# Late attention scores of two head pairs in one visit to the matrix engine's small tiles, and a second buffer for the gate's value

## The chip, the cores and the metric

The kernel runs on one core of one Trainium2 chip. A core has TensorE (PE in the profile: matmuls; PEld is its loading of weights), VectorE (DVE), ScalarE (ACT), GpSimd (POOL) and SyncE (SP), which here only issues transfers. Matmul results land in PSUM, which has eight banks; everything else lives in SBUF. The metric is the device time of one execution in microseconds.

## The reference

Attention over a sliding window of 96 keys plus 8 global ones, with a linear distance bias per head, followed by a two-layer network whose gate is a hard swish:

```python
batch, n_heads, seq, head_dim = (4, 8, 768, 64)
n_global, n_local = (8, 96)
scores = np.matmul(q, k.transpose(0, 1, 3, 2)) / np.sqrt(D)
scores = scores - slopes * dist            # masked unless global or local
a = np.exp(scores - max); a = a / (sum(a) + 1e-09)
x = (a @ v).transpose(0, 2, 1, 3).reshape(3072, 512)
h = x @ w_in                               # 512 x 2048
g = h * np.clip(h + 3.0, 0.0, 6.0) / 6.0
return g @ w_out                           # 2048 x 512
```

Everything is float32. The network's matmuls are made of three products each, of a high and a low part of both sides (names ending in h and l).

## The kernel before

The 3072 rows are eight blocks of 384 rows. A block has four head pairs (two heads side by side), so there are 32 pairs, n = 0 to 31. Attention of a block fills its x (xh, xl: four tiles, one for each pair), and the network then runs over 16 slices f of the hidden dimension: `first` (L172, 12 matmuls into a PSUM bank hp), `gate` (ACT makes g from hp, L183; DVE multiplies with hp, L184), `high` (POOL, or ACT in an early stage, rounds g to gh, L190 and L192), `rest` (DVE, gl = g - gh, L197), and `second` (L204, 9 matmuls, adding into three acc banks).

Up to some 150 us attention of blocks 0 to 2 and the network of blocks 0 and 1 go on while the network's weights are decoded: in steps on DVE (L433, L434, L442, L446, and L439, which writes the low parts w1l and w2l) and ACT (L399, L411, and L450, which writes w1h and w2h). Then comes a stage named "one", in which the third block's last three pairs are done ("late" pairs from here on, n = 9 and up), and the stage "layers": blocks 2 to 7 go through the network, each while attention for the next block is woven in.

The weave: `twos` takes two slices at a time: both `first` with their gates, two yields, both `second` of the slices before, two more yields. So a block has 32 yields, two for each half slice pair, and `attention` hangs work on their numbers ("units"). Unit k with k mod 4 of 0 or 1 stands after two `first`, with 2 or 3 after two `second`. `TURNS = (0, 5, 10, 16)` gives the unit at which each pair's scores are taken. At that unit `packed` runs: 24 matmuls (L877) in tiles of 64 x 32 of the array, into banks s and t (tiles sp, tp; one bank for each head), then for each of three row tiles and both heads `weigh`: DVE adds the bias and finds the least (L906), ACT takes the exponential with its sum (L910). At the same unit the next pair's queries are scaled (POOL, L863) and the load of the pair three further on is issued. Three units later come the sums' reciprocals (L920, L921) and `normalize` (POOL, L930), four and five later `spread` (DVE transposes into the one tile blocks, L952) and `send` (four transfers from blocks to weights, L958). Units 25 and 26 hold the two halves of `weighted`: attention times values (L704) for all four pairs of the block, into hp, xp, tp and sp, then x.

PSUM: three acc banks, two hp banks used in turn, one each of s, t and x. PE, SP and POOL run in the order in which the code is written; DVE's and ACT's order is set by a scheduler, from the dependencies. A buffer pool with one tile makes the next writer wait until the last reader is done; g has such a pool (`gp1`, one tile), and the scored rows n and their sums have one with three (`up`).

Of the kernel before, what the change touches and what calls it, by code (L numbers as in the profile page):

```python
# [9 lines left out]
F32 = mybir.dt.float32  # L10
# [9 lines left out]
P = 128  # L20
NT = 3
TB = NT * P
NTB = S // TB
NPAIR = H // 2
NKT = DM // P
NF = DF // P
BANK = 512
# [14 lines left out]
PW = PREV + NG + GQ  # L42
# [5 lines left out]
EARLY = 9  # L48
ROOMS = 3
TURNS = (0, 5, 10, 16)  # L50
LEAD = 6
# [12 lines left out]
class Kernel:  # L64
# [45 lines left out]
    def common(self, xs, banks):  # L110
        self.xp = self.pool("xp", xs)
        self.w1h, self.w1l, self.w2h, self.w2l = [], [], [], []
        self.gp = self.pool("gp", 4)
        self.lp = self.pool("lp", 3)
        self.gp1 = self.pool("gp1", 1)
        self.ps_h = self.pool("ps_h", banks, PSUM)
# [418 lines left out]
    def banded(self, flag):  # L535
# [12 lines left out]
        with ExitStack() as early, ExitStack() as words:  # L548
# [82 lines left out]
            self.decoded_to(2 * NF - 1)  # L631
        self.up = self.pool("up", 3, side="right")
        self.bp = self.pool("bp", 1, side="right")
# [9 lines left out]
        self.stage = "layers"  # L643
        x, ahead = xs[2], pairs[-1]
        for i in range(2, len(self.blocks)):
# [27 lines left out]
    def rest_of_third(self, x, slices):  # L673

        units = [[] for _ in range(2 * NF)]
        pairs = [Pair(self, n, x, False) for n in range(EARLY, 3 * NPAIR + 1)]
        pairs[0].scale()
        for p, (me, after) in enumerate(zip(pairs, pairs[1:])):
            at = units[3 * p + 1:]
            at[0] += [me.packed, after.scale, lambda me=me: self.load_next(me.n, False)]  # L680
            at[1] += [me.sum_up] + [lambda t=t, me=me: me.normalize(t) for t in range(NT)]
            at[2] += [lambda t=t, me=me: me.spread(t) for t in range(NT)] + [me.send]
        units[2 * slices - 1].append(lambda: list(self.weighted(pairs[:-1])))
        return units, pairs
# [25 lines left out]

    def attention(self, i, x, first):

        units = [[] for _ in range(2 * NF - 2)]
        pairs = [first]
        first.x = x
        for p in range(NPAIR):
            n = i * NPAIR + p
            me, after = pairs[p], Pair(self, n + 1, x, False) if n + 1 < len(self.blocks) * NPAIR else None
            pairs.append(after)
            at = units[TURNS[p]:]  # L720
            at[0] += [me.packed] + [a.scale for a in (after,) if a] + [lambda me=me: self.load_next(me.n, False)]
            at[3] += [me.sum_up, lambda me=me: me.normalize(0), lambda me=me: me.normalize(1)]
            at[4] += [lambda me=me: me.normalize(2), lambda me=me: me.spread(0)]
            at[5] += [lambda me=me: me.spread(1), lambda me=me: me.spread(2), me.send]
        values = self.weighted(pairs[:NPAIR])
        for k in (25, 26):
            units[k].append(lambda: next(values, None))
        return units, pairs[NPAIR]

# [111 lines left out]
class Pair:  # L841
# [22 lines left out]

    def packed(self):


        nc, kk = self.nc, self.k
        self.sums = kk.up.tile([P, 2, 2 * NT], F32, name="sums")
        banks = [kk.bank(b)[:, 0:NT * PW].rearrange("p (t c) -> p t c", t=NT) for b in "st"]  # L870
        keys, queries = kk.loaded(self.n)
        for t in range(NT):
            for g in range(GROUPS):
                own, c = slice(g * GQ, (g + 1) * GQ), t * TG + g * GQ
                for j in range(2):
                    rows = slice(j * D, (j + 1) * D)
                    nc.tensor.matmul(banks[j][own, t], lhsT=queries[rows, t, own], rhs=keys[rows, c:c + PW], start=True, stop=True,  # L877
                                     tile_position=(j * D, g * GQ))
        for t in range(NT):
            self.weigh(t, [bank[:, t] for bank in banks], kk.up.tile([P, 2, PW], F32, name="n"), 0)  # L880

    def scores(self, t):
# [10 lines left out]
        for j in range(2):  # L893
            rows = slice(j * D, (j + 1) * D)
            nc.tensor.matmul(sp[j][:, lo:W], lhsT=queries[rows, t], rhs=keys[rows, c], start=True, stop=True)  # L895
        return lambda: self.weigh(t, sp, e, lo)

    def weigh(self, t, sp, e, lo):
        nc, kk, end = self.nc, self.k, self.end
        for j in range(2):  # L900
            h, i = 2 * self.pr + j, 2 * t + j
            if self.plain:
                d, scale = (kk.p0 if lo else kk.p1)[:, h], PLAIN
            else:
                d, scale = kk.dl[:, 0 if self.first(t) else 1], SLOPES[h]
            nc.vector.tensor_tensor_reduce(out=e[:, j, lo:end], in0=sp[j][:, lo:end], in1=d, op0=ALU.add, op1=ALU.min, scale=scale,  # L906
                                           scalar=3.0e38, accum_out=self.least[:, i:i + 1])
        for j in range(2):
            i = 2 * t + j
            nc.scalar.activation(out=e[:, j, lo:end], in_=e[:, j, lo:end], func=AF.Exp, bias=self.least[:, i:i + 1], scale=-1.0,  # L910
                                 accum_out=self.sums[:, 0, i:i + 1])
        if self.n <= 2:
            kk.held = nc.cur_bb.bb.instructions[-1].name
        self.rows.append(e)

# [147 lines left out]
```

## Time and profile before

| | us |
|---|---|
| median of 3 runs (lowest, highest) | 646.46 (645.92, 646.66) |
| the profiled execution | 646.94 |
| its span, first to last instruction | 645.1 |
| PE busy | 634.7 |
| DVE busy | 355.0 |
| ACT busy | 255.2 |
| POOL busy | 167.4 |
| mean granted clock | 0.999 |

All times of rows are microseconds from the span's start. In a row of the timeline the start comes first, then the duration, the engine, the line, the operation, and what it writes and reads; in brackets stands how long its engine was idle before it and what ended that. In the table by stage, each engine's busy time stands for a stretch, with the number of instructions. Matmuls overlap, so a row's duration is longer than its step to the next row, and the start of one against the start of the next tells what it costs.

### The profile page before, as it was taken

The numbers are of one execution on the slowest core, as the hardware profiler recorded it, in microseconds if no ns is written. First come the engines' busy times: TensorE is split into PE (matmuls) and PEld (weight loads), VectorE is DVE, ScalarE is ACT, GpSimd is POOL, SyncE is SP. The second block draws the span as 40 slices with busy tenths as digits, with TensorE's granted clock in tenths as the row PEclk, the third lists the DMA queues.
The fourth block names the chain that finished last, engine by engine and source line by source line (L and its number), as shares of the span: only waits on it lengthen the run. The fifth ranks groups of instructions, "written<-read, shape, count | busy, mean of one in ns | idle before, by whom it ended". The sixth has DMA issues, their size and how long they took to land.

```text
span 645.1 us, 14438 instructions
## 1 busy us (share of the span) xinstructions
PE 634.7 (98%) x5593; PEld 559.6 (87%) x5593; DVE 355.0 (55%) x1066; ACT 255.2 (40%) x706; POOL 167.4 (26%) x371
## 2 busy tenths in 40 slices
PE   9989999999999999999999999999999999999997
PEld 7768999888888888988888889888889888899985
DVE  5889999996645552355524464245623555223222
ACT  5897877775415321242223232143212522221111
POOL 4668000000422441124302332033311242012100
PEclk9999999999999999999999999999999999999999
DMA  7675454543334421242232242123312311110001
GB/s 281 176 229 175 160 161 134 161 134 129 92 73 145 100 79 32 70 123 71 60 96 75 66 99 51 68 80 86 92 32 68 109 32 32 33 50 1 1 1 54
DMA packets 34334, 59.78 MB, mean 93 GB/s; under 512 B 3280, under 2 KB 21200, under 8 KB 33488
## 3 DMA queue, kind: packets, MB, share of 16 engines
q1 hardware_dynamic: 33968, 58.50, 30.8%
q8 instruction: 46, 0.75, 0.5%
q14 instruction: 32, 0.26, 0.1%
q10 hardware_dynamic: 288, 0.26, 0.1%
HBM read 41.16 MB, written 6.29 MB: 74 GB/s over the span
## 4 chain that ended last, share of the span: by engine, by line
PE 91%; DVE 2%; ACT 2%; DMA 1%; POOL 1%; issue 1%; SPq 0%; POOLq 0%; ACTq 0%; DVEq 0%
PE hp L172 41%; PE acc L204 36%; PE sp L877 2%; PE sp L204 2%; PE tp L204 1%; PE xp L204 1%; PE hp L704 1%; ACT n L910 1%; PE sp L704 1%; DMA wst<-w 1%; POOL n L930 1%; DMA load<-pairs 1%; PE xp L970 1%; PE sp L895 1%; PE tp L704 1%
## 5 line engine op out<-in xcount | busy, mean ns | idle before, releaser
L183 ACT ACTIVATE g<-hp,small 128x384 f32<-128x384 f32 x127 | 73.7, 580 | 259.6 <-PE hp L172 163.9
L172 PE MATMUL hp<-xh,w1h 128*128 128x384 f32 x512 | 173.7, 339 | 0.0
L172 PE MATMUL hp<-xh,w1l 128*128 128x384 f32 x512 | 172.4, 337 | 0.1
L172 PE MATMUL hp<-xl,w1h 128*128 128x384 f32 x512 | 171.7, 335 | 0.0
L190 POOL TENSOR_SCALAR gh<-g 128x384 fp32r<-128x384 f32 x104 | 53.6, 515 | 424.2 <-DVE g L184 397.3
L184 DVE SCALAR_TENSOR_TENSOR g<-g,hp 128x384 f32<-128x384 f32 x128 | 70.7, 552 | 121.0 <-ACT g L183 119.8
L204 PE MATMUL acc<-w2h,gh 128*128 128x512 f32 x336 | 133.2, 397 | 0.0
L204 PE MATMUL acc<-w2l,gh 128*128 128x512 f32 x336 | 131.7, 392 | 0.0
L204 PE MATMUL acc<-w2h,gl 128*128 128x512 f32 x336 | 131.7, 392 | 0.0
L197 DVE TENSOR_TENSOR gl<-g,gh 128x384 fp32r<-128x384 f32 x128 | 71.4, 558 | 78.5 <-POOL gh L190 58.8
L910 ACT ACTIVATE n<-n,least 128x136 f32<-128x136 f32 (+2 forms) x192 | 79.6, 417 | 54.1 <-DVE least L906 53.4
L172 PEld LDWEIGHTS hp<-xh,w1h 128*128 128x128 f32 x512 | 96.1, 188 | 4.7 <-issue 1.9
L172 PEld LDWEIGHTS hp<-xl,w1h 128*128 128x128 f32 x512 | 96.1, 188 | 2.6
L172 PEld LDWEIGHTS hp<-xh,w1l 128*128 128x128 f32 x512 | 96.1, 188 | 0.9 <-DVE w1l L439 0.8
L930 POOL TENSOR_SCALAR n<-n,sums 128x136 f32<-128x136 f32 (+2 forms) x186 | 82.4, 460 | 39.4 <-DVE sums L921 23.6
L204 PEld LDWEIGHTS acc<-w2h,gh 128*128 128x128 f32 x336 | 63.1, 188 | 15.6 <-issue 3.8
L204 PEld LDWEIGHTS acc<-w2h,gl 128*128 128x128 f32 x336 | 63.1, 188 | 13.8 <-DVE gl L197 0.3
L204 PEld LDWEIGHTS acc<-w2l,gh 128*128 128x128 f32 x336 | 63.1, 188 | 11.4
L952 DVE STREAM_TRANSPOSE blocks<-n 128x256 f32<-128x256 f32 x138 | 51.2, 424 | 22.9 <-POOL n L930 21.4
L910 ACT ACTIVATION_READ_ACCUMULATOR n<-n,least 128x1 f32 x192 | 36.2, 188 | 0.0
L399 ACT ACTIVATE wz<-wst 128x512 f32<-128x512 f32 x32 | 21.6, 677 | 6.1 <-DVE w2l L439 3.9
L446 DVE CUSTOM_DVE_ANT_0 wz<-wz,we 128x1024 uint16<-128x1024 uint16 x32 | 22.3, 696 | 1.3 <-POOL we L404 0.9
(126 smaller groups left out, 731.1 us busy)
## 6 DMA issues: line engine op xcount, KB each, us to landing
wst<-w SPq DMA_DIRECT2D x32, 512.0 KB, 3.6
load<-pairs SPq DMA_DIRECT2D x31, 444.0 KB, 3.5
weights<-blocks SPq DMA_DIRECT2D x92, 120.0 KB, 2.4
values<-values SPq DMA_DIRECT2D x6, 1024.0 KB, 4.9
out<-o SPq DMA_DIRECT2D x23, 256.0 KB, 2.4
values<-pairs SPq DMA_DIRECT2D x9, 384.0 KB, 3.9
out<-o ACTq DMA_DIRECT2D x1, 256.0 KB, 2.8
load<-pairs SPq DMA_DIRECT2D x1, 252.0 KB
```

Of the source, the lines that this page charges most:

```text
L172: self.nc.tensor.matmul(hp, lhsT=self.w1(w, f)[:, kt, :], rhs=a[:, kt, :], start=(n == 0), stop=(n == 3 * NKT - 1))
L183: nc.scalar.activation(out=g, in_=hp, func=AF.Relu, bias=self.three, scale=1.0)
L184: nc.vector.scalar_tensor_tensor(out=g, in0=g, scalar=6.0, in1=hp, op0=ALU.min, op1=ALU.mult)
L190: self.nc.gpsimd.tensor_scalar(out=gh, in0=g, scalar1=1.0, scalar2=0.0, op0=ALU.mult, op1=ALU.add)
L197: self.nc.vector.tensor_tensor(out=gl, in0=g, in1=gh.bitcast(F32), op=ALU.subtract)
L204: self.nc.tensor.matmul(acc[tt], lhsT=a[:, tk], rhs=self.w2(w, f), start=(f == 0 and j == 0), stop=(f == NF - 1 and j == 2))
L399: self.nc.scalar.activation(out=self.z[i].bitcast(F32), in_=words[:, :, 1].bitcast(F32), func=AF.Abs)
L446: tt(out=z, in0=z, in1=self.e.pop(i), op=ALU.add)
L704: nc.tensor.matmul(out[pr][j * D:(j + 1) * D, g0 * GQ:g1 * GQ], lhsT=self.values_of[own, c, j * D:(j + 1) * D], rhs=groups[own, j, g0:g1, ...
L910: nc.scalar.activation(out=e[:, j, lo:end], in_=e[:, j, lo:end], func=AF.Exp, bias=self.least[:, i:i + 1], scale=-1.0, accum_out=self.sums ...
L930: nc.gpsimd.tensor_scalar(out=e[:, j, lo:end], in0=e[:, j, lo:end], scalar1=over, scalar2=0.0, op0=ALU.mult, op1=ALU.add)
L952: nc.vector.transpose(out=self.blocks[:, :, t, 4 * s:4 * s + 4], in_=e[:, :, c:c + P].rearrange("p j (b q) -> p j b q", b=4))
```

## The change

`packed` is now called for two pairs in a row. `TURNS` is (2, 10): a block's pairs 0 and 1 at unit 2, pairs 2 and 3 at unit 10. The first of a couple writes an hp bank and the x bank, the second s and t; the first reads its hp bank for all three row tiles before its x bank (`heads`), in reductions and in exponentials. The first pair's normalize, spread and send keep their distance from the unit (3 to 5 later), the second's come two units after that. The queries of both pairs of a couple are scaled beforehand: the next couple's first at the unit of the scores, its second five units later. For that the third block's stage makes one more pair object and scales it. `up` has six tiles instead of three, and `gp1`, the gate's value, two instead of one.

```diff
@@ -47,7 +47,7 @@
 PLAIN = -1 / np.sqrt(D)
 EARLY = 9
 ROOMS = 3
-TURNS = (0, 5, 10, 16)
+TURNS = (2, 10)
 LEAD = 6
 WAKE = 9
 FIRST = 3
@@ -112,7 +112,7 @@
         self.w1h, self.w1l, self.w2h, self.w2l = [], [], [], []
         self.gp = self.pool("gp", 4)
         self.lp = self.pool("lp", 3)
-        self.gp1 = self.pool("gp1", 1)
+        self.gp1 = self.pool("gp1", 2)
         self.ps_h = self.pool("ps_h", banks, PSUM)
 
     def weight_chunk(self, i):
@@ -629,7 +629,7 @@
             for _ in self.halves(todo):
                 pass
             self.decoded_to(2 * NF - 1)
-        self.up = self.pool("up", 3, side="right")
+        self.up = self.pool("up", 6, side="right")
         self.bp = self.pool("bp", 1, side="right")
         self.late_tiles()
         self.op = self.pool("op", 3, side="right")
@@ -641,7 +641,7 @@
         self.finish()
         self.pending = []
         self.stage = "layers"
-        x, ahead = xs[2], pairs[-1]
+        x, ahead = xs[2], pairs[-2:]
         for i in range(2, len(self.blocks)):
             units, x_next = [], None
             if i + 1 < len(self.blocks):
@@ -673,14 +673,15 @@
     def rest_of_third(self, x, slices):
 
         units = [[] for _ in range(2 * NF)]
-        pairs = [Pair(self, n, x, False) for n in range(EARLY, 3 * NPAIR + 1)]
+        pairs = [Pair(self, n, x, False) for n in range(EARLY, 3 * NPAIR + 2)]
         pairs[0].scale()
-        for p, (me, after) in enumerate(zip(pairs, pairs[1:])):
+        for p, (me, after) in enumerate(zip(pairs[:-2], pairs[1:])):
             at = units[3 * p + 1:]
             at[0] += [me.packed, after.scale, lambda me=me: self.load_next(me.n, False)]
             at[1] += [me.sum_up] + [lambda t=t, me=me: me.normalize(t) for t in range(NT)]
             at[2] += [lambda t=t, me=me: me.spread(t) for t in range(NT)] + [me.send]
-        units[2 * slices - 1].append(lambda: list(self.weighted(pairs[:-1])))
+        at[4].append(pairs[-1].scale)
+        units[2 * slices - 1].append(lambda: list(self.weighted(pairs[:-2])))
         return units, pairs
 
     def weighted(self, pairs):
@@ -708,24 +709,26 @@
             self.put_x(pairs[0].x, pr, out[pr])
         self.load_values(block + 1)
 
-    def attention(self, i, x, first):
+    def attention(self, i, x, pairs):
 
         units = [[] for _ in range(2 * NF - 2)]
-        pairs = [first]
-        first.x = x
-        for p in range(NPAIR):
-            n = i * NPAIR + p
-            me, after = pairs[p], Pair(self, n + 1, x, False) if n + 1 < len(self.blocks) * NPAIR else None
-            pairs.append(after)
-            at = units[TURNS[p]:]
-            at[0] += [me.packed] + [a.scale for a in (after,) if a] + [lambda me=me: self.load_next(me.n, False)]
-            at[3] += [me.sum_up, lambda me=me: me.normalize(0), lambda me=me: me.normalize(1)]
-            at[4] += [lambda me=me: me.normalize(2), lambda me=me: me.spread(0)]
-            at[5] += [lambda me=me: me.spread(1), lambda me=me: me.spread(2), me.send]
+        for pair in pairs:
+            pair.x = x
+        pairs = pairs + [Pair(self, n, x, False) for n in range(i * NPAIR + 2, min(i * NPAIR + 6, len(self.blocks) * NPAIR))]
+        for p in range(0, NPAIR, 2):
+            couple, after = pairs[p:p + 2], pairs[p + 2:p + 4]
+            at = units[TURNS[p // 2]:]
+            at[0] += [lambda me=me, first=first: me.packed(first) for me, first in zip(couple, (True, False))]
+            at[0] += [a.scale for a in after[:1]] + [lambda me=me: self.load_next(me.n, False) for me in couple]
+            at[5] += [a.scale for a in after[1:]]
+            for k, me in enumerate(couple):
+                at[2 * k + 3] += [me.sum_up, lambda me=me: me.normalize(0), lambda me=me: me.normalize(1)]
+                at[2 * k + 4] += [lambda me=me: me.normalize(2), lambda me=me: me.spread(0)]
+                at[2 * k + 5] += [lambda me=me: me.spread(1), lambda me=me: me.spread(2), me.send]
         values = self.weighted(pairs[:NPAIR])
         for k in (25, 26):
             units[k].append(lambda: next(values, None))
-        return units, pairs[NPAIR]
+        return units, pairs[NPAIR:]
 
 
     def general_setup(self):
@@ -862,12 +865,13 @@
         _, q = kk.loaded(self.n)
         nc.gpsimd.tensor_scalar(out=q, in0=q, scalar1=kk.over[:, self.pr:self.pr + 1], scalar2=0.0, op0=ALU.mult, op1=ALU.add)
 
-    def packed(self):
+    def packed(self, first=False):
 
 
         nc, kk = self.nc, self.k
         self.sums = kk.up.tile([P, 2, 2 * NT], F32, name="sums")
-        banks = [kk.bank(b)[:, 0:NT * PW].rearrange("p (t c) -> p t c", t=NT) for b in "st"]
+        banks = [kk.ps_h.tile([P, BANK], F32, name="hp"), kk.bank("x")] if first else [kk.bank("s"), kk.bank("t")]
+        banks = [bank[:, 0:NT * PW].rearrange("p (t c) -> p t c", t=NT) for bank in banks]
         keys, queries = kk.loaded(self.n)
         for t in range(NT):
             for g in range(GROUPS):
@@ -876,8 +880,10 @@
                     rows = slice(j * D, (j + 1) * D)
                     nc.tensor.matmul(banks[j][own, t], lhsT=queries[rows, t, own], rhs=keys[rows, c:c + PW], start=True, stop=True,
                                      tile_position=(j * D, g * GQ))
-        for t in range(NT):
-            self.weigh(t, [bank[:, t] for bank in banks], kk.up.tile([P, 2, PW], F32, name="n"), 0)
+        self.rows = [kk.up.tile([P, 2, PW], F32, name="n") for _ in range(NT)]
+        for heads in ((0,), (1,)) if first else ((0, 1),):
+            for t in range(NT):
+                self.weigh(t, [bank[:, t] for bank in banks], self.rows[t], 0, heads)
 
     def scores(self, t):
         nc, kk = self.nc, self.k
@@ -893,11 +899,12 @@
         for j in range(2):
             rows = slice(j * D, (j + 1) * D)
             nc.tensor.matmul(sp[j][:, lo:W], lhsT=queries[rows, t], rhs=keys[rows, c], start=True, stop=True)
+        self.rows.append(e)
         return lambda: self.weigh(t, sp, e, lo)
 
-    def weigh(self, t, sp, e, lo):
+    def weigh(self, t, sp, e, lo, heads=(0, 1)):
         nc, kk, end = self.nc, self.k, self.end
-        for j in range(2):
+        for j in heads:
             h, i = 2 * self.pr + j, 2 * t + j
             if self.plain:
                 d, scale = (kk.p0 if lo else kk.p1)[:, h], PLAIN
@@ -905,13 +912,12 @@
                 d, scale = kk.dl[:, 0 if self.first(t) else 1], SLOPES[h]
             nc.vector.tensor_tensor_reduce(out=e[:, j, lo:end], in0=sp[j][:, lo:end], in1=d, op0=ALU.add, op1=ALU.min, scale=scale,
                                            scalar=3.0e38, accum_out=self.least[:, i:i + 1])
-        for j in range(2):
+        for j in heads:
             i = 2 * t + j
             nc.scalar.activation(out=e[:, j, lo:end], in_=e[:, j, lo:end], func=AF.Exp, bias=self.least[:, i:i + 1], scale=-1.0,
                                  accum_out=self.sums[:, 0, i:i + 1])
         if self.n <= 2:
             kk.held = nc.cur_bb.bb.instructions[-1].name
-        self.rows.append(e)
 
     def sum_up(self, t=None):
```

PE, at the first excursion of the stage "layers" (sp, tp, hp and xp are banks, load_72 and load_73 two pairs' keys and queries). Before:

```order
L172 MATMUL hp<-xh,w1l_145 128x384
L877 MATMUL sp<-load_72 32x136
L877 MATMUL tp<-load_72 32x136
...
L172 MATMUL hp<-xh,w1h_144 128x384
...
L877 MATMUL sp<-load_73 32x136
L877 MATMUL tp<-load_73 32x136
```

And now:

```order
L172 MATMUL hp<-xh,w1l_145 128x384
L881 MATMUL hp<-load_72 32x136
L881 MATMUL xp<-load_72 32x136
...
L881 MATMUL sp<-load_73 32x136
L881 MATMUL tp<-load_73 32x136
L172 MATMUL hp<-xh,w1h_144 128x384
```

The second pair's 24 matmuls follow the first's with no large matmul between.

DVE, at the end of the decoding, from the gate of slice 14 on (wz and we are the decoded chunk's tiles, w1l_1029 the low part of the first layer's weights for slice 15). Before:

```order
L433 TENSOR_SCALAR wz<-wz 128x512
L446 ISA wz<-wz,we 128x1024
L184 SCALAR_TENSOR_TENSOR g<-g,hp 128x384
L434 TENSOR_SCALAR wz<-wz 128x512
L439 TENSOR_TENSOR w1l_1029<-wz,w1h_1028 128x4x128
L442 SCALAR_TENSOR_TENSOR wz<-wst,wz 128x512
L197 TENSOR_TENSOR gl<-g,gh 128x384
```

And now:

```order
L184 SCALAR_TENSOR_TENSOR g<-g,hp 128x384
L446 ISA wz<-wz,we 128x1024
L433 TENSOR_SCALAR wz<-wz 128x512
L197 TENSOR_TENSOR gl<-g,gh 128x384
L434 TENSOR_SCALAR wz<-wz 128x512
L439 TENSOR_TENSOR w1l_1029<-wz,w1h_1028 128x4x128
L442 SCALAR_TENSOR_TENSOR wz<-wst,wz 128x512
```

The gate and gl stand ahead of decoding steps that they stood behind.

DVE, at the end of a block's attention (the last pair's transposes into blocks, then the gates of the slices up to the block's x, which `weighted` ends). Before:

```order
L184 SCALAR_TENSOR_TENSOR g<-g,hp 128x384
L197 TENSOR_TENSOR gl<-g,gh 128x384
L952 STREAM_TRANSPOSE blocks<-n 128x2x128 x2
L184 SCALAR_TENSOR_TENSOR g<-g,hp 128x384
L197 TENSOR_TENSOR gl<-g,gh 128x384
L184 SCALAR_TENSOR_TENSOR g<-g,hp 128x384
L197 TENSOR_TENSOR gl<-g,gh 128x384
L159 TENSOR_TENSOR xl<-hp,xh 128x384
```

And now:

```order
L197 TENSOR_TENSOR gl<-g,gh 128x384
L958 STREAM_TRANSPOSE blocks<-n 128x2x128 x2
L184 SCALAR_TENSOR_TENSOR g<-g,hp 128x384
L197 TENSOR_TENSOR gl<-g,gh 128x384
L184 SCALAR_TENSOR_TENSOR g<-g,hp 128x384
L197 TENSOR_TENSOR gl<-g,gh 128x384
L184 SCALAR_TENSOR_TENSOR g<-g,hp 128x384
L197 TENSOR_TENSOR gl<-g,gh 128x384
L184 SCALAR_TENSOR_TENSOR g<-g,hp 128x384
L197 TENSOR_TENSOR gl<-g,gh 128x384
L159 TENSOR_TENSOR xl<-hp,xh 128x384
```

Between the last transposes and x stand four gates instead of two.

## The prediction

> **What bounds the kernel now.** I read the page's busy shares and costliest groups first, then the table by stage, then TensorE's rows one by one, start against start.
>
> ```profile
> span 645.1 us, 14438 instructions
> PE 91%; DVE 2%; ACT 2%; DMA 1%; POOL 1%; issue 1%; SPq 0%; POOLq 0%; ACTq 0%; DVEq 0%
> L172 PE MATMUL hp<-xh,w1h 128*128 128x384 f32 x512 | 173.7, 339 | 0.0
> 198.00:570.00 372.00, 372.00 (x3800) 328.50 (x3799) 176.20 (x581) 109.41 (x352) 101.54 (x219) 1.00 0.27 71
> ACT g L183 <- DVE gl L197: 77.7, 39, 2.9
> ```
>
> From 198 to 570 us, where the change mainly acts, TensorE (PE) is busy for all 372 us at full clock; VectorE (DVE), ScalarE (ACT) and GpSimd (POOL) are at half or less. So only what shortens PE's own sequence counts. The last row is what the second g tile removes: 77.7 us of ACT waiting for gl. It pays nothing by itself, since PE waits for none of it.
>
> A modelled busy row hides short holes, so I compare starts.
>
> **Term 1, the merged excursions.** These are starts of a slice pair (594.44 to 602.75 without scores, 267.66 to 277.05 with one pair's scores), then the first and last score rows and the next large matmul.
>
> ```profile
> 594.44 0.33 PE L172 MATMUL hp<-xh,w1h 128*128 128x384 f32 x1
> 602.75 0.33 PE L172 MATMUL hp<-xh,w1h 128*128 128x384 f32 x1
> 267.66 0.33 PE L172 MATMUL hp<-xh,w1h 128*128 128x384 f32 x1
> 277.05 0.33 PE L172 MATMUL hp<-xh,w1h 128*128 128x384 f32 x1
> 271.94 0.30 PE L877 MATMUL sp<-load 64*32 64x136 f32 x1
> 272.63 0.28 PE L877 MATMUL tp<-load 64*32 64x136 f32 x1
> 272.84 0.50 PE L204 MATMUL acc<-w2h,gh 128*128 128x512 f32 x1
> 257.42:259.26 1.84, 1.84 (x130) 1.80 (x129) 0.00 (x0) 0.00 (x1) 0.00 (x0) 1.00 0.00 0
> ```
>
> A pair of slices takes 8.31 us, with scores 9.39: an excursion costs 1.08. Its 48 records (24 matmuls, two each) begin between 271.94 and 272.63, 0.69 us; the other 0.39 is entry and exit. A second pair that follows at once in free banks needs the 0.69 and no entry or exit. That the pace holds for twice as long I take from the value matmuls: some 128 records in 1.84 us, 14 ns each, as in a score burst (0.69/48). The twenty late pairs become ten excursions: 10 x 0.39 = **-3.9 us**. The other end: the second pair costs the full distance from first score to next large matmul, 0.90; then 1.08 - 0.90 = 0.18 is saved, 1.8 in all. I take 3.9, since nothing stands between the two pairs: no wait on PE, banks hp, xp, sp and tp all free.
>
> A rule speaks against this term. The Trainium skill, page "TensorEngine Tiling (Array Packing)", section Instruction Overhead, gives each matmul some 60 cycles however short it is; at the 2.4 GHz of "Trainium Kernel Development and Optimization", NeuronCore Architecture, that is 25 ns, my estimate for 48 records in a row is 1.2 us, more than an excursion now, and the merge would lose 0.1 each time, 1 us in all. The trace's 14 ns do not agree: the eight array tiles overlap.
>
> **Term 2, the values' wait.** Per block, the values' matmuls come as two bursts, after units 25 and 26. The first:
>
> ```profile
> 232.59 0.30 PE L877 MATMUL sp<-load 64*32 64x136 f32 x1
> 245.53 0.77 DVE L952 STREAM_TRANSPOSE blocks<-n 128x256 f32<-128x256 f32 x2 [0.56 <-POOL n L930]
> 246.33 2.56 SPq L958 DMA_DIRECT2D weights<-blocks  x4
> L704 PEld LDWEIGHTS sp<-weights,values x32: 127/131/133, 250.8 to 252.8; 32*64 32x64 f32 x32
> L704 PEldq EVENT_SEMAPHORE  x1: 706/706/706, 250.1 to 250.1; - x1
> 250.31 0.54 PE L704 MATMUL tp<-weights,values 32*64 32x384 f32 x2
> 250.87 0.54 PE L704 MATMUL sp<-weights,values 32*64 32x384 f32 x2
> 326.10:328.45 2.35, 2.35 (x97) 1.92 (x97) 1.04 (x2) 0.58 (x1) 0.41 (x1) 1.00 0.00 1
> 332.80:334.42 1.62, 1.62 (x114) 1.58 (x113) 0.00 (x0) 0.01 (x1) 0.00 (x0) 1.00 0.00 0
> 190.57:193.82 3.25, 3.25 (x158) 2.89 (x157) 0.48 (x1) 0.00 (x0) 0.00 (x0) 1.00 0.03 5
> ```
>
> The fourth pair's matmuls (tile sp) start 0.56 us after the third's (tp), where 0.02 would do; PE's sequencer sat 0.71 in a wait. What came late is that pair's send: its last transposes end at 246.30, the four DMAs are issued from 246.33 and land some 4.5 us behind the transposes, at 250.8. Second witness: 13 chunks take 3.25 us in the one burst at 190.57 (three pairs, but the tiles of all pairs run side by side, so a chunk takes as long), and 2.35 + 1.62 = 3.97 in the two at 326.10 and 332.80; a second exit is 0.2 (272.63 to 272.84), so 0.5 is the wait. Now the fourth pair's scores stand at unit 10, not 16. From that excursion to the values' first burst lie 1.8 + 3 x 8.31 + 4.2 = 30.9 us instead of 17.7 (232.59 to 250.3); its spread and send come at units 16 and 17, behind only the slices 8 and 9 gates, and by the chain below land near 23 us: 8 to spare. Five blocks x 0.5 = **-2.5 us** (ends 1.5, if the chunks behind the wide one absorb part, and 3.0).
>
> **Term 3, the decode's last slices.** Until 152 us DVE both decodes weights and serves the gates, almost without a gap. The second g tile lets the scheduler set some gates earlier in DVE's order, and decoding steps move with them.
>
> ```profile
> PEld hp L172 <- DVE w1l L439: 0.8, 2, 0.4
> 136.77 0.34 PE L172 MATMUL hp<-xl,w1h 128*128 128x384 f32 x1
> 137.18 0.44 PE L172 MATMUL hp<-xh,w1l 128*128 128x384 f32 x1
> 147.60 0.58 ACT L183 ACTIVATE g<-hp,small 128x384 f32<-128x384 f32 x1 [1.00 <-PE hp L172]
> 148.19 0.62 ACT L450 CAST w1h<-wz 128x512 fp32r<-128x512 f32 x1
> 147.13 0.42 DVE L433 TENSOR_SCALAR wz<-wz 128x512 f32<-128x512 f32 x1
> 147.47 0.68 DVE L446 CUSTOM_DVE_ANT_0 wz<-wz,we 128x1024 uint16<-128x1024 uint16 x1
> 148.21 0.56 DVE L184 SCALAR_TENSOR_TENSOR g<-g,hp 128x384 f32<-128x384 f32 x1
> 148.68 0.42 DVE L434 TENSOR_SCALAR wz<-wz 128x512 int32<-128x512 int32 x1
> 149.02 0.69 DVE L439 TENSOR_TENSOR w1l<-wz,w1h 128x512 fp32r<-128x512 f32 x1
> 149.44 0.34 PE L172 MATMUL hp<-xh,w1h 128*128 128x384 f32 x1
> ```
>
> PE waits twice for w1l today (slices 10 and 13), 0.8 in the row, 0.24 by the matmul starts 136.77 and 137.18 where 0.17 is the step; I take 0.35 each. In the new order both w1l stand ahead of gl or of a decode step (0.5 to 0.6 us): **-0.7**. For slice 15 it turns over. The gate of slice 14 now stands ahead of the decode step L446; it cannot begin before ACT's g ends (148.18), so DVE, whose L446 began at 147.47, now idles till then, runs g to 148.68 (0.47 from start to start) and L446 to 149.37; the cast w1h on ACT (0.62) follows: w1h is there near 150.0 instead of 148.8, while PE wants it at 149.44, 0.6 late. w1l now comes behind L446, L433, gl and L434 (0.6, 0.34, 0.47, 0.34 by starts, gl taken as long as g) and ends near 151.1 against 149.71; PE, already 0.6 behind, wants it two matmuls later, at 150.4: another 0.7. **+1.3** (ends: 0, if DVE's chain starts enough earlier than PE's, and 2).
>
> **Edits costed at nothing.** The same 23 query scalings (POOL), loads, sends and reductions are issued, only elsewhere. On SP two loads go in a row ahead of eight sends; the sends wait for transposes anyway. What is new is a long ACT and DVE job per excursion: twelve reductions and twelve exponentials, behind which both gates stand.
>
> ```profile
> 276.37 1.54 ACT L60 ACTIVATE o<-acc 128x512 f32<-128x512 f32 x3
> L910 ACT ACTIVATE n<-n,least 128x136 f32<-128x136 f32 (+2 forms) x192 | 79.6, 417 | 54.1 <-DVE least L906 53.4
> 303.52 2.57 POOL L930 TENSOR_SCALAR n<-n,sums 128x136 f32<-128x136 f32 x6
> L952 DVE STREAM_TRANSPOSE blocks<-n 128x256 f32<-128x256 f32 x138 | 51.2, 424 | 22.9 <-POOL n L930 21.4
> 273.61 0.29 DVE L906 CUSTOM_DVE_ANT_0 n<-sp,dl 128x136 f32<-128x136 f32 x1
> 273.82 0.29 DVE L906 CUSTOM_DVE_ANT_0 n<-tp,dl 128x136 f32<-128x136 f32 x1
> ```
>
> From the first excursion's start: three o copies on ACT to 1.6, twelve exponentials at 0.4 to 6.4, sums and both gates on DVE to 7.9. The next slice that wants the gate's bank starts at 1.8 + 8.3 = 10.1 us: 2.2 to spare. Then on POOL two gh and six n (2.57) to 11.6, transposes to 12.2; the first pair's send frees the blocks tile 4.5 later, 16.7; the second pair's six transposes (0.37 apart by the rows above) with a gate and a gl between end near 19.9. Only then DVE reads the scores of the second excursion, which began at 18.4. Its hp bank is read first, three reductions of 0.22, done at 20.6; the slice that wants that bank starts at 18.4 + 1.8 + 2.1 = 22.3. Cover 1.7 us, in each block's second excursion; without it, every us beyond costs five.
>
> **Sum.** -3.9 - 2.5 - 0.7 + 1.3 = -5.8 us. The profiled execution took 646.94 us (1.8 of it outside the span), so 641.1; the median of the runs, 646.46, lies 0.48 below it, so I forecast **640.7 us**.
>
> **Rivals.**
> - *The second pair of an excursion does not run at the first one's pace* (0.90 instead of 0.69): 1.8 saved, 642.8 us. For it: nowhere in the trace do 96 such score records follow each other. Against it: the long value bursts keep 14 ns. Chance 0.10. By the rule of the page on tiling, an estimate, the time would end near 645.7; since 14 ns per record is measured, I leave it 0.01 of the 0.10.
> - *The wait ahead of the fourth pair's values stays*, because something other than the send ends it: 640.7 + 2.5 = 643.2. For it: the row names no releaser. Against it: the send's end and the wait's end agree to a tenth. Chance 0.10.
> - *DVE's new order costs more*: two further gates (slices 9 and 12) also moved ahead; if each held decode up as slice 14's does, +2.6, 643.3. Against it: of sixteen w1l the wait row above names two, so the others have slack now. Chance 0.08.
> - *The other side: the second excursion's hp bank comes free late.* DVE is in order: the second pair's first transpose waits for the first pair's send, and gates, reductions and PE stand behind it. It decides from 1.7 us of lateness; from 1.7 + 5.8/5 = 2.9 us it eats the whole gain. Were a send to need 8 us instead of 4.5, it would cost 5 x 1.8 = 9: 649.7. For it: the loads and the next sends share SP's queue. Against it: the four DMAs of a block's pair took the same 4.5 us in the row above. Chance 0.05.
> - *The change moves nothing on PE* (banks or scalings not ready, the couple split again): 646.5. PE's order speaks against it. Chance 0.03.
>
> **How the numbers follow.** My own case has the remaining 0.64, with a range from 639.5 (no new decode wait, value wait 0.6) to 642. The range 639.5 to 643.4 takes in the first three rivals. 0.2% (1.3 us) is about what a measurement of this kernel tells from no change: faster than 645.2 are my case and the first three rivals, 0.92; within it the last, and a milder bank wait, 0.04; slower than 647.7 is the bank rival, 0.04.
>
> **What the profile after would show.** Ten late excursions, their score rows about 1.4 us from first to last; slice-pair starts 8.31 + 1.79 apart around them (a 2.0 means the first rival). The value bursts 2.35 and 2.75 shrink to some 1.85 and 2.25, the sequencer's wait at L704 is gone. No w1l wait near 115 and 136 us, but one near 149, 1.3 together on w1h and w1l. No PE hole two slices after a block's second excursion: such a hole, on DVE's reductions, would make the prediction wrong, and so would sends that land after 30 us.

## Result and the profile after

The changed kernel takes 642.80 us (median of 4 runs, 641.78 to 643.03) against 646.42: a ratio of 0.9937, 95% interval 0.9924 to 0.9949, so 3.6 us less. The forecast was 640.7, from 639.5 to 643.4: right in sign and within the range, 2.1 us too low. The profiled execution took 643.03 with a span of 641.2, 3.9 less than the 645.1 before; the forecast was 5.8 less.

Two rows of the page of the changed kernel, one of its table by stage, and two of its list of waits:

```profile
span 641.2 us, 14374 instructions
L172 PE MATMUL hp<-xh,w1h 128*128 128x384 f32 x512 | 174.2, 340 | 0.5 <-ACT w1h L450 0.5
```

```profile
198.00:570.00 372.00, 372.00 (x3829) 332.91 (x3828) 176.57 (x583) 108.91 (x354) 103.99 (x219) 1.00 0.26 72
```

```profile
ACT g L183 <- PE hp L172: 252.4, 91, 5.7
DVE blocks L958 <- DMA weights<-blocks: 22.4, 11, 2.4
```

PE is still busy throughout the stage; it now starts more matmuls in the same 372 us (3829 against 3800). ACT's gate no longer waits for gl at all (89.5 us in the whole execution before), and but for one wait of 2.0 us for POOL it waits for PE alone. Two things are new: an idle time of PE for w1h, and DVE's transposes waiting 22.4 us for sends (1.5 before).

The merged excursion, from the timeline (first score, first and last of the second pair, next large matmul, and the starts of the slice pairs around two excursions):

```profile
267.66 0.33 PE L172 MATMUL hp<-xh,w1h 128*128 128x384 f32 x1
276.06 0.30 PE L881 MATMUL hp<-load 64*32 64x136 f32 x1
276.78 0.28 PE L881 MATMUL sp<-load 64*32 64x136 f32 x1
277.47 0.28 PE L881 MATMUL tp<-load 64*32 64x136 f32 x1
277.67 0.44 PE L172 MATMUL hp<-xh,w1h 128*128 128x384 f32 x1
286.09 0.33 PE L172 MATMUL hp<-xh,w1h 128*128 128x384 f32 x1
```

The second pair follows without a gap and takes 0.69 us, as the first; first to last score are 1.41 us. From 267.66 to 286.09 are two slice pairs and one excursion: 18.43 = 2 x 8.31 + 1.81. Two single excursions cost 2.16, so one merged saves 0.35, and ten save 3.5.

The values' first bursts, in the table by stage, in the rows of L705 (L704 before) and in PE's timeline:

```profile
250.72:253.07 2.35, 2.35 (x130) 1.89 (x129) 1.03 (x2) 0.58 (x1) 0.51 (x1) 1.00 0.00 0
325.40:327.41 2.01, 2.01 (x97) 1.55 (x96) 1.04 (x2) 0.58 (x1) 0.51 (x1) 1.00 0.00 0
```

```profile
L705 PEld LDWEIGHTS sp<-weights,values x32: 127/131/132, 250.8 to 252.8; 32*64 32x64 f32 x32
L705 PEldq EVENT_SEMAPHORE  x8: 51/51/51, 247.5 to 250.5; - x8
250.76 0.54 PE L705 MATMUL sp<-weights,values 32*64 32x384 f32 x2
```

The sequencer's 706 ns are gone, and sp starts with the other three tiles (hp, the first of them, at 250.72). The first bursts take 2.35, 2.01, 2.35, 2.01 and 2.35 us instead of 2.79, 2.35, 2.73, 2.38 and 2.74: 1.9 in all.

Slice 15 of the decode, in the timelines of DVE, ACT and PE:

```profile
147.94 0.55 DVE L184 SCALAR_TENSOR_TENSOR g<-g,hp 128x384 f32<-128x384 f32 x1 [0.60 <-ACT g L183]
148.41 0.68 DVE L446 CUSTOM_DVE_ANT_0 wz<-wz,we 128x1024 uint16<-128x1024 uint16 x1
149.13 0.62 ACT L450 CAST w1h<-wz 128x512 fp32r<-128x512 f32 x1
149.80 0.45 PE L172 MATMUL hp<-xh,w1h 128*128 128x384 f32 x1 [0.47 <-ACT w1h L450]
150.16 0.68 DVE L439 TENSOR_TENSOR w1l<-wz,w1h 128x512 fp32r<-128x512 f32 x1
150.89 0.44 PE L172 MATMUL hp<-xh,w1l 128*128 128x384 f32 x1 [0.48 <-DVE w1l L439]
```

As forecast, DVE idles for ACT's g, L446 slips behind the gate, w1h and then w1l come late, and PE stands twice.

Since PE runs the network's matmuls in the same order in every kernel here, the start of the same matmul in two traces says where time went. From the slice that starts at 115.37 us before to the one at 198.08 (82.71 us), the changed kernel needs 0.83 more; from there to the last slice's start (198.08 to 633.27, 435.19 us) it needs 429.82, so 5.37 less. The rest, 0.6, is lost ahead of 115 us (0.3) and behind the last slice's start (0.4), which the forecast did not touch. The first of these two is one late transfer, in ACT's timeline:

```profile
52.46 0.66 ACT L399 ACTIVATE wz<-wst 128x512 f32<-128x512 f32 x1 [2.20 <-DMA wst<-w]
```

Here ACT waits 2.20 us for raw weights, and PE falls 0.7 behind (of which it had been 0.4 ahead). The same wait is 2.5 and 2.6 in two of the kernels below, 0.5 to 1.3 in five, and absent in four and before. Up to this row ACT, DVE and POOL have their instructions in the same order in all of these kernels, and two kernels that both have two g tiles from the start have the wait short and long (0.5 in two_g_alone, 2.6 in two_banks), so I take it for a matter of the execution. It was not tried by itself.

### The profile page after: what moved, and what is told of

Its sections match the earlier page's. It is cut to its first block, busy times and chain, and to the rows that moved or that the text cites. A ratio compares the mean times of both kernels' runs of the same rounds, so it can differ in the third digit from the quotient of the medians.

```text
span 641.2 us, 14374 instructions
## 1 busy us (share of the span) xinstructions
PE 628.5 (98%) x5593; PEld 557.5 (87%) x5593; DVE 354.1 (55%) x1066; ACT 253.7 (40%) x706; POOL 169.8 (26%) x371
## 4 chain that ended last, share of the span: by engine, by line
PE 90%; DVE 4%; ACT 2%; DMA 2%; POOL 1%; issue 1%; POOLq 0%; ACTq 0%
PE hp L172 42%; PE acc L204 36%; PE sp L204 2%; PE tp L204 2%; PE xp L204 2%; PE hp L705 1%; ACT n L917 1%; PE hp L881 1%; DVE n L913 1%; DMA wst<-w 1%; PE xp L705 1%; DMA iv<-bounds 1%; POOL n L936 1%; PE tp L705 1%; PE tp L881 1%
## 5 line engine op out<-in xcount | busy, mean ns | idle before, releaser
L204 PE MATMUL acc<-w2h,gh 128*128 128x512 f32 x336 | 131.6, 392 | 0.0
L184 DVE SCALAR_TENSOR_TENSOR g<-g,hp 128x384 f32<-128x384 f32 x128 | 69.4, 548 | 99.4 <-ACT g L183 98.4
L197 DVE TENSOR_TENSOR gl<-g,gh 128x384 fp32r<-128x384 f32 x128 | 73.8, 582 | 76.5 <-POOL gh L190 39.2
L936 POOL TENSOR_SCALAR n<-n,sums 128x136 f32<-128x136 f32 (+2 forms) x186 | 84.3, 473 | 17.2 <-DVE sums L927 12.3
L958 DVE STREAM_TRANSPOSE blocks<-n 128x256 f32<-128x256 f32 x138 | 51.6, 422 | 31.9 <-DMA weights<-blocks 22.4
L446 DVE CUSTOM_DVE_ANT_0 wz<-wz,we 128x1024 uint16<-128x1024 uint16 x32 | 22.1, 692 | 1.4 <-POOL we L404 0.9
```

The source lines that it names most:

```text
L184: nc.vector.scalar_tensor_tensor(out=g, in0=g, scalar=6.0, in1=hp, op0=ALU.min, op1=ALU.mult)
L197: self.nc.vector.tensor_tensor(out=gl, in0=g, in1=gh.bitcast(F32), op=ALU.subtract)
L204: self.nc.tensor.matmul(acc[tt], lhsT=a[:, tk], rhs=self.w2(w, f), start=(f == 0 and j == 0), stop=(f == NF - 1 and j == 2))
L446: tt(out=z, in0=z, in1=self.e.pop(i), op=ALU.add)
L936: nc.gpsimd.tensor_scalar(out=e[:, j, lo:end], in0=e[:, j, lo:end], scalar1=over, scalar2=0.0, op0=ALU.mult, op1=ALU.add)
L958: nc.vector.transpose(out=self.blocks[:, :, t, 4 * s:4 * s + 4], in_=e[:, :, c:c + P].rearrange("p j (b q) -> p j b q", b=4))
```

## Experiments

Each kernel was profiled once and timed. Columns: median; ratio to the kernel before, which was timed anew beside each group (medians 646.64, 647.12 and 646.67), with its 95% interval; then, from starts of the same matmuls in its profile, the length of the end of decoding (115.37 to 198.08 before) and of the stretch with the late excursions (198.08 to 633.27 before).

| kernel | us | ratio | end of decoding | late stretch |
|---|---|---|---|---|
| before | 646.46 | 1 | 82.71 | 435.19 |
| changed | 642.80 | 0.9937 (0.9924 to 0.9949) | 83.54 | 429.82 |
| one_g | 642.61 | 0.9935 (0.9918 to 0.9952) | 82.68 | 430.88 |
| two_g_alone | 646.05 | 0.9991 (0.9979 to 1.0002) | 83.56 | 433.18 |
| turn14 | 645.36 | 0.9976 (0.9966 to 0.9986) | 82.71 | 433.29 |
| split | 646.03 | 0.9990 (0.9981 to 1.0000) | 83.57 | 433.67 |
| g2_late | 641.80 | 0.9922 (0.9909 to 0.9935) | 82.74 | 430.06 |
| one_g_wide | 642.93 | 0.9938 (0.9925 to 0.9951) | 82.69 | 431.39 |
| two_banks | 664.45 | 1.0282 (1.0261 to 1.0303) | 83.58 | 450.66 |
| one_burst | 649.67 | 1.0042 (1.0026 to 1.0057) | 82.73 | 435.96 |
| one_g_212 | 641.64 | 0.9924 (0.9911 to 0.9938) | 82.72 | 429.82 |
| g2_late_212 | 641.50 | 0.9923 (0.9910 to 0.9937) | 82.74 | 429.59 |
| heads_together | 642.47 | 0.9936 (0.9922 to 0.9949) | 83.55 | 430.10 |

The fourth column reads by itself: five of five kernels with two g tiles during decoding lose 0.83 to 0.87 us there, and the seven others lose nothing.

**split: the merging undone.** Changed kernel, with

```
-            at[0] += [lambda me=me, first=first: me.packed(first) for me, first in zip(couple, (True, False))]
+            at[0] += [lambda me=couple[0]: me.packed(True)] + ...
+            at[2] += [lambda me=couple[1]: me.packed(False), ...]
```

> The changed kernel with a couple's second pair scored two units later (after the next two firsts instead of right behind the first pair), its load with it; banks, sums, normalize, spread and send stay where they are. Theory: ten entries and exits of the small tiles come back at 0.35 each: +3.5 against the changed kernel, 646.3; a slice pair with its excursion is again 8.31 + 1.08 long, and the score rows 0.69 from first to last. The value bursts stay as in the changed kernel. Rival: the merging itself saves little (0.1 to 0.18 each, the other end of my term), and the gain comes from earlier sends: 644 to 644.6. If nothing hangs on the merging, 642.8.

```profile
269.12 0.33 PE L172 MATMUL hp<-xh,w1h 128*128 128x384 f32 x1
287.90 0.33 PE L172 MATMUL hp<-xh,w1h 128*128 128x384 f32 x1
```

These are the starts around two slice pairs with two single excursions, in its timeline: 18.78 us against the changed kernel's 18.43. The late stretch is 3.85 longer, of which 0.4 is a wait for a g behind the very first excursion, so 3.4 belongs to the merging: ten times 0.34. By the two ratios to the kernel before it is 0.0053 of that time, 3.4 us. The theory holds; the other end (1.8 in all) does not. The bursts are those of the changed kernel (2.35 and 2.01).

**turn14: the last pair's send earlier, nothing merged.** Kernel before, with

```
-TURNS = (0, 5, 10, 16)
+TURNS = (0, 5, 10, 14)
...
-        self.up = self.pool("up", 3, side="right")
+        self.up = self.pool("up", 6, side="right")
```

> The kernel before with its last pair's scores at unit 14 instead of 16 (and six tiles instead of three for n and sums, which the overlap of two pairs needs), so that its send goes out at unit 19 instead of 21, some 4 us earlier. No pairs are merged. Theory: the values' wait was for that send; PE's sequencer wait at L704 goes and each block's first burst is 0.38 us shorter, 5 x 0.38 = 1.9 us less: 644.5. Rival: the wait is ended by something else (the values' load, the hp bank): the 0.71 stays and the time is 646.4.

The late stretch is 1.90 shorter, the first bursts are 2.35 and 2.01, and all semaphore waits of L704 in the first block's values are 51 ns. By the runs it is 0.9976, 1.6 us less. The values' wait was for that send.

**two_g_alone: the second g tile without the rest.** Kernel before, with

```
-        self.gp1 = self.pool("gp1", 1)
+        self.gp1 = self.pool("gp1", 2)
```

> The kernel before with two tiles for the gate's value, nothing else. Theory: +1.4 at slice 15 and -0.5 at slices 10 and 13, nothing after 198 us: 0.9 us slower than before, 647.3. Rival: two tiles help PE in the stage from 198 to 570 us (ACT waits 77.7 us for gl there): faster than before by over 1 us. Third way: the stall near 51 to 54 us belongs to it: 648.

Both halves of the table were needed to read it. The end of decoding is 0.85 longer, as the theory has it, but the late stretch is 2.01 shorter, which the theory had at zero. The rows of L704, and two of DVE's timeline, say where:

```profile
L704 PEld LDWEIGHTS sp<-weights,values x32: 128/131/132, 251.1 to 253.1; 32*64 32x64 f32 x32
L704 PEldq EVENT_SEMAPHORE  x8: 51/51/184, 247.8 to 250.8; - x8
```

```profile
243.44 0.56 DVE L184 SCALAR_TENSOR_TENSOR g<-g,hp 128x384 f32<-128x384 f32 x1 [0.19 <-ACT g L183]
245.81 0.77 DVE L952 STREAM_TRANSPOSE blocks<-n 128x256 f32<-128x256 f32 x2 [0.28 <-POOL n L930]
```

The wait for the fourth pair's values is 184 ns instead of 706, the burst 2.34 instead of 2.79. PE is 0.75 behind the kernel before at that place, yet the last transposes begin only 0.28 later: the second gate no longer waits for the first gl, POOL gets to gh and n earlier, and the send leaves some half a microsecond earlier against PE. So two parts of the change remove the same wait, and either is enough.

**one_g: the changed kernel with one g tile.**

```
-        self.gp1 = self.pool("gp1", 2)
+        self.gp1 = self.pool("gp1", 1)
```

> The changed kernel with one tile for the gate's value instead of two; the merged excursions and the new turns stay. Theory: the second tile only moves gates in the decode and pays nothing later. Then the wait at slice 15 (1.4 us near 147 to 152 us) goes, the two waits for w1l at 115 and 136 us (0.25 each) come back, and the stage from 198 to 570 us keeps its length: 0.9 us less than the changed kernel, some 641.9. Rival: the second tile is what lets both gates behind twelve exponentials finish in time; with one, the second g waits for the first gl, and PE stalls some 0.5 us two slices after each of ten excursions: +5, some 647, with idle time of PE on DVE g (L184) there. Third way: the stall near 51 to 54 us (0.7 us, ACT waiting for a load of weights) hangs on the second tile too; then 641.2.

The 0.86 of the decode come back, and 1.06 are lost in the late stretch: together nothing. So the theory misses the late stretch, and the rival misses size and place. The loss is in the first two blocks. PE's timeline, DVE's and the waits, at the first block's second excursion (scores from 218.56):

```profile
218.92 0.45 DVE L958 STREAM_TRANSPOSE blocks<-n 128x256 f32<-128x256 f32 x1 [2.25 <-DMA weights<-blocks]
221.55 0.77 DVE L958 STREAM_TRANSPOSE blocks<-n 128x256 f32<-128x256 f32 x2 [0.28 <-POOL n L936]
222.25 0.26 DVE L913 CUSTOM_DVE_ANT_0 n<-hp,dl 128x136 f32<-128x136 f32 x1
222.66 0.29 DVE L913 CUSTOM_DVE_ANT_0 n<-hp,dl 128x136 f32<-128x136 f32 x1
222.20 0.34 PE L172 MATMUL hp<-xh,w1l 128*128 128x384 f32 x1
223.10 0.41 PE L172 MATMUL hp<-xh,w1h 128*128 128x384 f32 x1 [0.57 <-DVE least L913]
```

This is the chain of the prediction's rival of the other side: the second pair's transposes wait for the first pair's send, DVE reads the excursion's hp bank only behind them (the last of three reductions ends at 222.95), and PE, which would want the bank at 222.4, goes on at 223.10. It costs 0.7 and 0.3 in two blocks. The changed kernel has no such hole, but two g tiles alone don't rule it out: g2_late and heads_together below have one each. What the changed kernel has to spare there, from the last reduction's end to the slice that takes the bank, is 0.57 and 0.71 in these two blocks and 1.7, 1.7 and 1.6 in the other three; the prediction had 1.7 in each.

**one_g_wide and one_g_212: is it the distance of the excursions?** one_g with

```
-TURNS = (2, 10)
+TURNS = (0, 10)        # one_g_wide
+TURNS = (2, 12)        # one_g_212
```

> The changed kernel with one g tile throughout and TURNS (0, 10) instead of (2, 10): the two excursions of a block stand ten units apart instead of eight, 4.2 us more. Theory: the holes of one_g come from the first couple's first send (DVE's transposes of the second pair wait 2.2 us for it, and the reductions that free the excursion's hp bank stand behind them); with 4.2 us more the send has landed, both holes (1.2 in sum) go, and PE's starts gain that against one_g: some 641.4. Rival: the holes come from the gates behind twelve exponentials with one g tile, which the distance does not touch: 642.6 as one_g.

That missed. The second block's hole is gone, but the first block's grew. At the first block no `second` is pending, so units 0 and 2 are the same place of PE's order and its two excursions stand no further apart (199.89 and 218.50). And there DVE's timeline shows another chain:

```profile
217.73 2.08 DVE L958 STREAM_TRANSPOSE blocks<-n 128x256 f32<-128x256 f32 x6 [4.02 <-DMA weights<-blocks]
219.73 0.51 DVE L197 TENSOR_TENSOR gl<-g,gh 128x384 fp32r<-128x384 f32 x1
220.95 0.56 DVE L184 SCALAR_TENSOR_TENSOR g<-g,hp 128x384 f32<-128x384 f32 x1 [0.71 <-ACT g L183]
```

All six transposes wait 4.02 us for the send, gl stands behind them, ACT's g waits for gl (one tile), and PE waits 1.4 us for g. Hence the second try, which leaves the first excursion where it was:

> The changed kernel with one g tile throughout and TURNS (2, 12): the first excursion stays where it is, the second comes after the next two firsts, so that the slice which wants its hp bank is some 4 us further off (5.5 us of cover by one_g_wide's excursions at such a place, against 0.15 in one_g's first two blocks). Theory: one_g's holes are the hp bank of the second excursion, freed late because DVE's reductions stand behind transposes that wait for a send; they go in both blocks, 1.2 in sum: PE's starts at 631 us some 1.2 earlier than in one_g, the time some 641.4, and a second g tile is worth nothing any more. Rival, from one_g_wide, whose first block lost 1.4 us to a gl that stood behind those transposes: with one g tile the gate chain itself waits for the send, wherever the excursion is; then a hole near 220 us stays, on g or gl, and the time is 642.6.

Both holes are gone: the late stretch is 1.06 shorter than one_g's, 429.82, as long as the changed kernel's, and the time 641.64. The holes were a matter of distance; with it, the second g tile is worth 0.2 in this stretch (429.59 in g2_late_212 below).

**g2_late: two g tiles, but only behind the decoding.** Changed kernel, with a second pool opened at the stage "one" and the two used in turn:

```
-        self.gp1 = self.pool("gp1", 2)
+        self.gp1 = [self.pool("gp1", 1)]
...
-        g = self.gp1.tile([P, TB], F32, name="g")
+        self.gp1 = self.gp1[::-1]
+        g = self.gp1[0].tile([P, TB], F32, name="g")
...
         self.up = self.pool("up", 6, side="right")
+        self.gp1.append(self.pool("gp2", 1, side="right"))
```

> The changed kernel with one g tile while weights are decoded, and the second g tile only from the stage named one on. Theory: the second tile costs 0.85 us net in the decode (PE's starts at the last decoded slices: +1.4 at slice 15, -0.5 at slices 10 and 13; the same in two_g_alone) and pays some 1.1 after 198 us, where with one tile (one_g) PE stands 0.8 and 0.4 two slices after the second excursions of the first two blocks. So both are to be had: 0.85 less than the changed kernel, some 641.9, with no wait at 147 to 152 us and no such holes. Rival: the order that a scheduler makes in the layers depends on the decode before it, the holes come back: 642.6.

As the theory had it: the decode's loss is gone (82.74), the late stretch nearly kept (430.06), 641.8 us. One hole remains, 0.5 by the starts around it, at the first block's second excursion, again on the hp bank.

**g2_late_212: the hole taken away.** g2_late with TURNS (2, 12).

> g2_late with TURNS (2, 12). Theory: g2_late keeps one hole, 0.55 us near 222 us in the first block, again on the second excursion's hp bank (its cover there is 0.16, in the later blocks 0.7 to 1.7); with the second excursion two units later it goes: some 641.2, and PE's starts at 631 us 0.5 earlier than in g2_late. Rival: the last pair's send, now at unit 19, is late for the values, as in the kernel before: 0.38 a block come back, 643.

The late stretch is 429.59, 0.47 less, and the first bursts stay at 2.35 and 2.00, so a send at unit 19 is early enough. 641.50 us is the lowest median of all; against the changed kernel's 0.9937 the ratio of 0.9923 has an interval that overlaps, so the runs alone don't part the two. In the traces, decode and late stretch together are 1.0 us shorter. Nor do they part it from one_g_212 (0.9924), which has no second g tile at all and is 0.2 us longer by its trace.

**two_banks: both pairs of a couple in s and t.** Changed kernel, with `zip(couple, (False, False))`.

> The changed kernel with both pairs of a couple in banks s and t, as the pairs of the kernel before, so the second pair's matmuls wait until DVE has read the first pair's scores. Theory: at a block's first excursion six reductions of 0.22 and their start keep PE some 1.1 us; at its second one DVE comes to the scores only after the transposes that wait for the send, some 2 to 3 us after PE: 3.1 to 4.2 a block, five blocks 16 to 21, so 658 to 664. Rival: matmuls and reductions of different row tiles overlap far enough that the wait is a few tenths: 644 to 646.

```profile
283.73 0.39 PE L881 MATMUL sp<-load 64*32 64x136 f32 x2 [1.39 <-DVE least L913]
```

Every second pair waits for the first one's reductions: excursions take 3.4 (a block's first; 4.7 the very first) and 3.7 us instead of 1.61. 664.45 is just above the theory's end. Without four banks the merge costs six times what it saves (20.8 us of the late stretch against 3.5).

**heads_together: the hp bank not read first.** Changed kernel, with

```
-        for heads in ((0,), (1,)) if first else ((0, 1),):
+        for heads in ((0, 1),):
```

> The changed kernel with the first pair of a couple read row tile by row tile, both heads of each, as the second one is, so that its hp bank is free three reductions (0.66 us) later. Covers read from the changed kernel (last reduction of the hp bank to the slice that wants it): 2.07 at first excursions, 0.57 and 0.71 at the second ones of the first two blocks, 1.4 to 1.7 later. Theory: 0.1 us is lost in the first block, 0.3 at most in all, the time stays 642.8 to 643.1. Rival: the order was what kept PE going, a hole of some 0.6 at every second excursion: 645.8.

The covers shrink as reckoned: 1.63 at first excursions (0.40 in the first block), 0.16 and 0.28 at the second ones of the first two blocks; PE stands 0.2 us once. The late stretch is 0.28 longer and the time is the same within what the runs can tell. The order of reading is a margin, not a gain.

**one_burst: the same idea on the values.** g2_late with `units[26].append(lambda: list(values))` instead of halves at units 25 and 26.

> g2_late with a block's values in a single burst at unit 26 instead of two at 25 and 26. Theory: what a burst costs beside its matmuls is entry and exit of the small tiles, as with the excursions; the two bursts take 2.35 + 1.84 or 2.01 + 1.62 and leave 0.12 in the second that follows; one burst saves some 0.4 to 0.5 a block, 2.0 to 2.5 us in all: some 639.6 if g2_late is 641.9. Rival: the first burst's length is the wide chunk's own (its records come 0.34 apart), nothing is entry or exit, and the time is g2_late's.

Slower by 0.0042, and 7.9 us above g2_late (5.9 of it in the late stretch): neither the theory's time nor the rival's. PE's timeline in the first block (the starts of tile hp's first three steps, then the hole), and the queues within 257 to 258 us:

```profile
254.44 0.54 PE L707 MATMUL hp<-weights,values 32*64 32x384 f32 x2
254.81 0.49 PE L707 MATMUL hp<-weights,values 32*64 32x384 f32 x2
255.13 0.19 PE L707 MATMUL hp<-weights,values 32*64 32x32 f32 x2
257.70 0.24 PE L707 MATMUL hp<-weights,values 32*64 32x96 f32 x1
259.58 0.24 PE L707 MATMUL hp<-weights,values 32*64 32x96 f32 x1 [1.61 <-issue]
```

```profile
q8 instruction: 1, 0.02, 5.5%
```

After 210 matmul records in 3.3 us PE stands 1.61 us, released by nothing that the profile shows ("issue"). In all five bursts such a hole of 1.15 to 1.61 us comes after 188 to 218 records. A packet of the instruction queue (q8) starts 0.8 to 1.3 us ahead of each of the five holes; in g2_late it starts 0.1 to 0.6 us behind the end of each burst. That fits a PE that has run out of fetched instructions; this cause was not tried.

What the joining itself is worth depends on how a hole is counted. From the last start before it to the first behind it (257.70 to 259.58 in the first block), the holes take 1.39 to 1.88, 7.8 in sum; the late stretch is only 5.9 longer, so all the rest is 1.9 shorter, 0.39 a block. That is the low end of the theory's 0.4 to 0.5, and about as much as an excursion's entry and exit. If PE's idle time alone counts (6.65), it is 0.8 in all. The starts are the better measure, since matmuls overlap: so joining does save an entry and an exit, as the theory had it, and the hole costs four times that. The rival is right that the wide first chunk is long: its two steps take 0.37 and 0.32 in the rows above.

## Why the prediction was right or wrong

- **Term 1, merging: mechanism right, 0.04 of 0.39 too large.** The second pair costs 0.72 from first score to first score, not 0.69 (0.03 more), and 0.01 is rounding of starts: -3.5 instead of -3.9, confirmed by split with 3.4. The rival of the slower second pair (0.90, and a 2.0 between slice pairs) is ruled out by 1.81. That its 642.8 is the measured time is chance: the missing microseconds lie elsewhere. The rule of the Trainium skill, page "TensorEngine Tiling (Array Packing)", section Instruction Overhead, of some 60 cycles for each matmul, would make 96 records last 2.4 us by my estimate; 1.41 were measured, so it does not hold for these tiles side by side.
- **Term 2, the values' wait: right place and cause, 0.38 instead of 0.5 a block.** The step that failed is the comparison of 13 chunks in one burst and in two as the wait's price. It let a chunk of three pairs last as long as one of four: in one_burst's second block 13 chunks of four pairs take 3.41 in one burst (4.82 less the hole's 1.42 by starts) instead of 3.25, so some 0.16 of the 0.5 was work, not wait. -1.9 instead of -2.5. And the credit was given to the turns alone: two_g_alone shows that the second g tile removes most of this wait by itself. "It pays nothing by itself, since PE waits for none of it" was wrong: ACT's wait for gl reached PE through POOL, the transposes and the send. I judged the 77.7 us by who waits next, not by the end of the chain.
- **Term 3, the decode: right, row by row.** -0.5 instead of -0.7 at slices 10 and 13, +1.4 instead of +1.3 at slice 15; two_g_alone and four more kernels repeat the sum of 0.85.
- **Edits costed at nothing: right for this kernel, with less cover than given.** First excursions had 2.07 to spare (2.2 forecast) but 0.84 in the first block; second ones 1.7 in the later blocks (1.7 forecast) but 0.57 and 0.71 in the first two. There DVE waits 2.3 and 2.2 us for the send, later 1.7 to 1.8. The working took one block for all.
- **Sum.** -3.5 - 1.9 - 0.5 + 1.4 = -4.5, and +0.7 from a late transfer of weights and the end of the span, which no term had: -3.8, against the 3.9 measured in the span. The start at 115 us and the end of the span differ by as much between the kernels here (114.94 to 115.97, and 11.67 to 12.25 behind the last slice's start), so these 0.7 say little of the change. The measured 642.80 also lies above 642, the end of the range of my own case: it is inside the forecast only by the room that was left for rivals, none of which came about.

## What to carry to other kernels

An excursion to small array tiles has a price for going there and back that can be shared, but only if free banks let the second job follow without a wait: the same merge gained 3.4 us with four banks, and with two the kernel was 18 us slower than before. A second buffer is bought per stage: here it let a scheduler reorder a stage where the vector engine was full, which cost what it gained later. Giving it only to the later stage kept the gain without the cost, and moving the second excursion further off gained as much without the buffer. When several edits remove one wait, try each alone before crediting either, and follow an off-path wait through every in-order queue behind it before calling it free.

## What was not expected of the hardware

A run of short matmuls has a limit that no wait row names: after 188 to 218 records in 3.1 to 3.4 us PE stood 1.15 to 1.61 us with the mark "issue", in five of five bursts, while bursts of up to 128 records in 2.35 us, 156 in 3.24 (at 190.57 us in the kernel before), and 96 score records in 1.41 had no such hole.
